# A fused recurrence and two expert mixtures: the first mixture's low weight halves and the logits' penalty moved from GpSimd to VectorE

## The chip, the core and the metric

One core of a Trainium2 chip runs the whole program as one launch. The metric is the device time of the launch in microseconds (us), as the median of several runs. Engines are named as the profile names them: PE is the matmul engine (TensorE) and PEld its weight loads, DVE is VectorE, ACT is ScalarE, POOL is GpSimd, SP is SyncE.

## The reference

Three stages work on 20224 tokens of 256 values, in float32.

```python
# 1. a gated recurrence over each of 4 sequences of 5056
f = lower_bound + (1 - lower_bound) * sigmoid(f_logit)
h = f[:, t] * h + (1 - f)[:, t] * x[:, t];  y[:, t] = h
# 2. first mixture: 8 experts, each takes exactly cap = 2528 tokens,
#    greedily by the sorted logits x @ w_gate
out[mask] = relu(x[mask] @ w1[e]) @ w2[e]          # w1: 256x1024, w2: 1024x256
# 3. second mixture: tokens with x @ w_skip > 0, each to its best expert
out[do] = xc + softmax_weight * (relu(xc @ w1[e]) @ w2[e])
```

## The kernel before

**Stages.** `attention` (L371) computes the recurrence and the first router's logits `L`, one value per token and expert. The first mixture follows, then the second. Each runs its experts one after the other.

**Split weights.** Every float32 weight is split into a high half, which is the value rounded to the matmul's format and is copied by ACT, and a low half, which is the value minus the high half. A product is three matmuls: high by high, low by high and high by low. The raw weights of one expert lie in `w1r` and `w2r`. The halves lie in two alternating sets, w10h, w10l, w20h, w20l and w11h, w11l, w21h, w21l, one for even and one for odd experts. `split_w` (L568) makes them in eight steps, four for w1 and four for w2, each of one ACT copy and one subtraction of 128x512. Its argument names the engine of the subtraction, but L579 sets it to POOL for the last four steps:

```python
        for h in range(DH):
            for c in range(0, F, F // 2):
                ...
                split_pool(w1h[:, h, s], w1l[:, h, s], w1r[:, h, s])
        eng = nc.gpsimd
        for a in range(0, FB, 2):
            split_pool(w2h[:, a:a + 2, :D], w2l[:, a:a + 2, :D], w2r[:, a:a + 2])
```

**Tiles of the first mixture.** An expert's tokens are five tiles of up to 512. A tile has eight slots `f` of 128 hidden values. In each slot, `up` (L875) issues six matmuls of 512 columns into a bank `hp`. ACT makes the high half `hh` of the relu, DVE the low half `hl`, which is the last reader of the bank. There are two such banks, so the `up` two slots later waits for this `hl`. `down` (L893) issues 12 matmuls for the slot two before. `gather` fetches the next tile's tokens with four indirect DMAs from POOL's queue, and after each tile `disp2` sends its rows out with eight indirect DMAs (`scatter`) from the same queue.

**Routing beside the tiles.** `route(k)` (L675) finds which tokens expert k takes, while expert k-1 computes. At its end it loads the expert's raw weights, takes the tokens out (`pn`, `apen`, `dl`), adds a large negative penalty to the chosen expert's logits (`L`, L796, one POOL instruction of 128x1264, for k below 6) and turns the choice into row numbers: `mstep` on DVE, three matmuls, then `cc`, `idf` and `idx`.

**Order.** The program is straight-line for each engine. What is interleaved goes by an estimate of when each engine gets to its work (class `Paced`). `route`, `prepare_w` (L836, the splits of expert k's weights, then `fold`, L843, which puts the second router's columns behind w2) and `prepare_2` (L827, the second mixture's first weights) are generators that yield conditions. `offer` (L929) goes on with each as long as `fits` says yes: a condition ("D", x) wants DVE's estimated end plus x to be at most PE's plus 3.0 us, ("A", x) the same for ACT with 1.0 us, ("R", t) wants t written. `prepare_w` asks for ("A", 0.5) and the raw weights, and for nothing of POOL. `until` (L1099) forces the generators on where a tile needs what they make. The first expert's weights are split before the first tile by `split_w(0, nc.vector)` (L1064). In the second mixture `ahead` (L1328) splits with `nc.gpsimd`.

Almost all of this stage is recorded under one line, L109, the pacing wrapper's, so the profile is read by tile names.

Of the kernel before, what the change touches and what calls it, by code (L numbers as in the profile page):

```python
# [20 lines left out]
class Paced:  # L21
    """nc, with an estimate of when each engine gets to what it was given: what is interleaved goes by it"""

# [18 lines left out]
    def look(self, table, ap):  # L42
        """the latest of the times that the table has for what overlaps ap"""
        lo, hi = self.span(ap)
        return max((t for (a, b), t in table.get(ap.name, {}).items() if a < hi and lo < b), default=0.0)
# [9 lines left out]
    def slot(self, tag, n, ap):  # L55
        """the tile ap takes the place of the one that had the tag n tiles ago"""
        old = self.banks.setdefault(tag, [])
        if len(old) >= n:
            self.book(self.w, ap[:], max(self.look(self.w, old[-n]), self.look(self.r, old[-n])))
        old.append(ap[:])  # L60
# [54 lines left out]
def attn_moe_moe2(ctx, tc, x, f_logit, lower_bound, g1, w1a, w2a, sk, g2, w1b, w2b, out):  # L115
# [35 lines left out]

# [1 line left out]
    jp = consts.tile([P, P], I32)  # L153
# [120 lines left out]
    def pick(a, b, k):  # L274
        """m: each token's best logit among the experts left, V: that one at its expert, else very low"""
        s = slice(a, b)
        n = b - a
        bc = [P, n, E]
        w8 = wE[:, None, :].to_broadcast(bc)
        nc.vector.tensor_reduce(m[:, s], L[:, s], axis=AX.X, op=OP.max)  # L280
        yield
        nc.vector.tensor_tensor(eqw[:, s], L[:, s], m[:, s, None].to_broadcast(bc), op=OP.is_equal)
        yield
        nc.vector.tensor_tensor(eqw[:, s], eqw[:, s], w8, op=OP.mult)
        yield
        nc.vector.tensor_reduce(ch[:, s], eqw[:, s], axis=AX.X, op=OP.max)
        if k:
            nc.vector.tensor_tensor(m[:, s], m[:, s], apen[:, s], op=OP.min)
        yield
        nc.vector.tensor_tensor(eqw[:, s], w8, ch[:, s, None].to_broadcast(bc), op=OP.not_equal)  # L290
        yield
        nc.vector.scalar_tensor_tensor(V[:, s], eqw[:, s], -2.0 * BIG, m[:, s, None].to_broadcast(bc),
                                       op0=OP.mult, op1=OP.add)
# [10 lines left out]
    def vt(g0, g1_, pt):  # L304
        """V's columns g0 * CG to g1_ * CG, experts along the partitions"""
        full = 0
        for g in range(g0, g1_):
            n = min(CG, C - g * CG)
            full += n == CG
            nc.tensor.transpose(pt[:n * E, (g - g0) * P:(g - g0 + 1) * P],  # L310
                                V[:, g * CG:g * CG + n, :].rearrange("p c e -> p (c e)"), ident)
        if full:
            nc.scalar.activation(VT[:, g0 * P:(g0 + full) * P], pt[:, :full * P], AF.Copy)
        if full < g1_ - g0:
            r = (C - (g1_ - 1) * CG) * E
            nc.scalar.activation(VT[:r, (g1_ - 1) * P:g1_ * P], pt[:r, full * P:(full + 1) * P], AF.Copy)

    def counts(v, TG):
        """how many of each partition's values reach the two values of TG"""
        n = v.free_size()  # L320
        cnt = rs.tile([P, 2], FT, name="cnt")
        nc.vector.tensor_scalar(junkd[:, :n], v, TG[:, 0, 0:1], 0.0, op0=OP.is_ge, op1=OP.add,
                                accum_out=cnt[:, 0:1])
        nc.scalar.activation(junka[:, :n], v, AF.Sign, bias=TG[:, 1, 0:1], scale=-1.0, accum_out=cnt[:, 1:2])
        return cnt
# [8 lines left out]
    def weigh(pc, rh, kc, LH, TG):  # L334
        """the fullest expert's count beside each value, and the ends LH moved to them"""
        pc3 = pc[:, :3 * E].rearrange("p (i e) -> p i e", i=3)
        nc.tensor.matmul(pc[:, :3 * E], ones, rh.rearrange("p i e -> p (i e)"), start=True, stop=False)
        nc.tensor.matmul(pc[:, :3 * E], ones, kc.rearrange("p i e -> p (i e)"), start=False, stop=True)
        nc.vector.tensor_reduce(TG[:, :, 1], pc3, axis=AX.X, op=OP.max)
        mk = rs.tile([P, 2, 2], I32, name="mk")  # L340
        nc.vector.tensor_scalar(mk[:, :, 0], TG[:, 0:2, 1], 0.0, None, op0=OP.is_ge)
        nc.vector.tensor_scalar(mk[:, :, 1], TG[:, 1:3, 1], 0.0, None, op0=OP.is_lt)
        for i in range(2):
            nc.vector.copy_predicated(LH, mk[:, i, :, None].to_broadcast([P, 2, 2]), TG[:, i:i + 2])

    def aim(LH, ca, cb):
        """the next two values: where a line between the ends would meet the wanted count, and a bit aside"""
        w = rs.tile([P, 1], FT, name="w")
# [12 lines left out]
    def ends(LH):  # L361
        """the first two values"""
        TG = rs.tile([P, 3, 2], FT, name="TG")
        nc.vector.tensor_copy(TG[:, 0::2, 0], LH[:, 0, 0:1].to_broadcast([P, 2]))
        dd = rs.tile([P, 1], FT, name="dd")
        nc.vector.tensor_tensor(dd, LH[:, 1, 0:1], LH[:, 0, 0:1], op=OP.subtract)
        nc.vector.scalar_tensor_tensor(TG[:, 1, 0:1], dd, -0.3, LH[:, 1, 0:1], op0=OP.mult, op1=OP.add)
        return TG
# [5 lines left out]
    def attention():  # L374
        with tc.tile_pool(name="a_in", bufs=3) as ain, tc.tile_pool(name="a_w", bufs=2) as aw, \
# [68 lines left out]
            def early(a, b):  # L444
                """the tokens' best experts, as far as they are known"""
                yield from pick(a, b, 0)
# [7 lines left out]
            def sample(b):  # L454
                """the first threshold as the first b columns would have it, and how far it may be off"""
                yield
# [111 lines left out]
    def split_w(q, eng):  # L568
# [5 lines left out]
        for h in range(DH):  # L574
            for c in range(0, F, F // 2):
                s = slice(c, c + F // 2)
                split_pool(w1h[:, h, s], w1l[:, h, s], w1r[:, h, s])
                yield
        eng = nc.gpsimd  # L579
        for a in range(0, FB, 2):  # L580
            split_pool(w2h[:, a:a + 2, :D], w2l[:, a:a + 2, :D], w2r[:, a:a + 2])
            yield

# [1 line left out]
    routed = {}  # L585
# [7 lines left out]
    def narrow(LH, tf, tiles, i):  # L593
        """one more value between the ends, on VectorE alone"""
        Z, Zt, Y, W, Wt, q, qi, c8, d1, mk = tiles
# [26 lines left out]
    def settle(LH):  # L622
        """where the rounds were not enough: some more, and then bit by bit"""
        tiles = [rs.tile([P, 32], FT, name="fZ", bufs=1), rs.tile([P, 32], FT, name="fZt", bufs=1),
# [16 lines left out]
    def bits(tf, tiles):  # L641
        """the greatest threshold that leaves some expert full, bit by bit, on VectorE alone"""
        Z, Zt, Y, W, Wt, q, qi, c8, _, _ = tiles
# [31 lines left out]
    def route(k):  # L675
        """a generator: yields the point of a slot at which it goes on"""
        last = k == E - 1
# [111 lines left out]
        if not last:  # L789
# [5 lines left out]
            if k < E - 2:  # L795
                nc.gpsimd.tensor_tensor(L, L, dl[:, None, :].to_broadcast([P, C, E]), op=OP.add)  # L796
        cc = rs.tile([P, 2, NJ], FT, name="cc")
# [29 lines left out]
    def prepare_2():  # L827
        load_raw(w1b[0], w2b[0])
        yield [("W", lambda: at[0] >= (E - 1) * TN * FB + 2)]
        step = split_w(0, nc.gpsimd)  # L830
        for _ in range(8):
            yield [("A", 0.5), ("R", w2r)]
            next(step, None)
        load_raw(w1b[1], w2b[1])

    def prepare_w(k):  # L836
        step = split_w(k % 2, nc.gpsimd)
        for _ in range(8):
            yield [("A", 0.5), ("R", w2r)]
            next(step, None)  # L840
        yield from fold(k % 2)

    def fold(q):  # L843
        """the second router's columns behind w2"""
        w2h, w2l = wts[q][1]
# [20 lines left out]

# [1 line left out]
    def xsplit_h(src, nb, off, h, xs):  # L868
# [42 lines left out]

# [1 line left out]
    TN = (NJ + 3) // 4  # L913
# [189 lines left out]

# [1 line left out]
    KT = 12  # L1105
# [30 lines left out]
    def tables():  # L1136
        nc.vector.tensor_tensor(cnt, base[0:1], bf0, op=OP.subtract)
        nc.vector.tensor_scalar(nti, cnt, float(T2 - 1), None, op0=OP.add)
        nc.vector.tensor_scalar(nti, nti, T2.bit_length() - 1, None, op0=OP.logical_shift_right)
        # a rest of up to P rows goes along with an earlier tile  # L1140
        nc.vector.scalar_tensor_tensor(wd[:, 0], nti, -1.0 * T2, cnt, op0=OP.mult, op1=OP.add)
# [14 lines left out]
        yield  # L1156
        # s2: the tile after the next expert's first
        g = s12[:, 2, :E - 1]
# [6 lines left out]
        yield  # L1165
        # nx[e, j + 1]: the second tile after tile j of expert e
        bc = [1, E, KT + 1]
# [108 lines left out]
    def broad(e, j):  # L1276
        """body, with the expert's last P rows beside the tile's"""
        q = e % 2
# [55 lines left out]

    # the first expert's first two tiles, from what the tiles before the last one sent it
    mt = bank()
# [111 lines left out]
```

## Time and profile before

| | us |
|---|---|
| median of 3 runs | 1945.02 (1944.35 to 1946.91) |
| span of the profiled execution | 2129.3 |
| attention, to the first matmul of the first mixture's `up` | 251.3 |
| first mixture, seven experts up to the eighth's first `up` | 251.3 to 1411.9 |

The profiled execution's own span is 184.3 us above the median of the unprofiled runs. The page doesn't show where that difference lies. Busy times are by engine. An idle time stands in brackets in the timeline, ahead of the instruction that ended it, with what released it.

### The profile page before, as it was taken

How to read it: one execution, taken by the hardware profiler on the slowest of the kernel's cores; microseconds unless marked ns; L12 is line 12 of the kernel's file. 1: busy time of each engine (PE TensorE's matmuls, PEld its weight loads, DVE VectorE, ACT ScalarE, POOL GpSimd, SP SyncE). 2: the span in 40 equal slices, each digit the busy share in tenths (PEclk: the TensorE clock that was granted, in tenths of full speed). 3: DMA queues.
4: the chain of work that ended last, by engine and by line, in shares of the span. 5: the costliest groups of instructions: out<-in, count | busy, mean ns of one | idle time of the engine just before them, and what ended most of it. 6: DMA issues, size and time to landing. Idle time of an engine off the chain costs nothing. (4 is left out here: it accounts for less than half of the span.)

```text
span 2129.3 us, 34969 instructions
## 1 busy us (share of the span) xinstructions
PE 1808.8 (85%) x12538; PEld 1663.9 (78%) x12538; DVE 1131.0 (53%) x3142; ACT 753.8 (35%) x1703; POOL 838.7 (39%) x847
## 2 busy tenths in 40 slices
PE   7994398898788789888797889888989999998998
PEld 6884277787677688777686778877879989998998
DVE  8999666666565666666565534332333333333332
ACT  4664243433433333433333443232222322223321
POOL 4552233542624443542634446354351322314311
PEclk9998699898889899998899999989999999999999
DMA  8999210212101110210201222011022323323222
GB/s 277 299 305 308 81 38 30 71 31 66 33 29 40 61 40 29 71 33 28 73 28 39 68 72 78 28 54 59 30 78 81 106 67 101 92 84 122 62 68 60
DMA packets 154181, 176.76 MB, mean 83 GB/s; under 512 B 17822, under 2 KB 129332, under 8 KB 153920
## 3 DMA queue, kind: packets, MB, share of 16 engines
q1 hardware_dynamic: 126800, 120.85, 18.8%
q0 software_dynamic: 27120, 52.76, 7.7%
q8 instruction: 124, 2.03, 0.4%
q14 instruction: 137, 1.12, 0.2%
HBM read 118.71 MB, written 76.34 MB: 92 GB/s over the span
## 5 line engine op out<-in xcount | busy, mean ns | idle before, releaser
L109 DVE SCALAR_TENSOR_TENSOR hl<-hp,hh 128x512 fp32r<-128x512 f32 (+2 forms) x480 | 322.8, 673 | 590.8 <-ACT hh L109 463.3
L109 ACT ACTIVATE hh<-hp 128x512 fp32r<-128x512 f32 (+2 forms) x480 | 280.4, 584 | 808.8 <-PE hp L109 581.7
L109 POOL DMA_INDIRECT buf_scr<-rt,ix x160 | 164.0, 1025 | 588.7 <-ACT hh L109 337.4
L109 PE MATMUL op<-w21h,hh 128*128 128x266 f32 (+1 forms) x960 | 262.4, 302 | 36.3 <-ACT rt L109 22.6
L109 PE MATMUL op<-w20h,hh 128*128 128x266 f32 (+1 forms) x960 | 261.9, 301 | 35.7 <-ACT rt L109 15.6
L109 PE MATMUL op<-w21l,hh 128*128 128x266 f32 (+1 forms) x960 | 255.6, 294 | 1.4 <-issue 1.4
L109 PE MATMUL op<-w20l,hh 128*128 128x266 f32 (+1 forms) x960 | 255.4, 294 | 0.0
L109 PE MATMUL hp<-xsh,w10h 128*128 128x256 f32 (+3 forms) x624 | 224.3, 369 | 29.2 <-DVE hl L109 13.7
L109 PE MATMUL hp<-xsh,w11h 128*128 128x512 f32 (+3 forms) x616 | 218.7, 365 | 27.8 <-DVE hl L109 21.5
L109 POOL DMA_INDIRECT out_dram<-xg,tin x85 | 83.7, 985 | 392.8 <-DVE xg L109 324.6
L109 PEld LDWEIGHTS op<-w21h,hh 128*128 128x128 f32 x960 | 189.7, 198 | 46.8 <-ACT rt L109 25.0
L109 PEld LDWEIGHTS op<-w20h,hh 128*128 128x128 f32 x960 | 189.4, 197 | 44.4 <-issue 19.6
L109 PE MATMUL hp<-xsh,w10l 128*128 128x256 f32 (+3 forms) x624 | 214.3, 353 | 0.4 <-issue 0.4
L109 PE MATMUL hp<-xsh,w11l 128*128 128x512 f32 (+3 forms) x616 | 210.0, 350 | 0.0
L109 PEld LDWEIGHTS op<-w21l,hh 128*128 128x128 f32 x960 | 189.7, 198 | 5.4 <-issue 0.8
L109 PEld LDWEIGHTS op<-w20l,hh 128*128 128x128 f32 x960 | 189.7, 198 | 5.0
L109 POOL DMA_INDIRECT xg<-y_scr,idx x160 | 167.5, 1047 | 59.9 <-issue 46.1
L109 POOL DMA_INDIRECT out_dram<-rt,ix x160 | 158.1, 988 | 48.8 <-issue 48.2
L109 PE MATMUL hp<-xsl,w10h 128*128 128x256 f32 (+3 forms) x624 | 167.7, 350 | 2.5 <-DVE txi L109 1.5
L109 PE MATMUL op<-w20h,hl 128*128 128x266 f32 (+1 forms) x960 | 164.0, 294 | 3.4 <-issue 3.3
L109 PE MATMUL op<-w21h,hl 128*128 128x266 f32 (+1 forms) x960 | 163.2, 294 | 1.9 <-issue 1.8
L109 PE MATMUL hp<-xsl,w11h 128*128 128x512 f32 (+3 forms) x616 | 164.0, 348 | 0.0
(372 smaller groups left out, 3543.1 us busy)
## 6 DMA issues: line engine op xcount, KB each, us to landing
ft<-in_f_logit_dram SPq DMA_DIRECT2D x39, 512.0 KB
xt<-in_x_dram SPq DMA_DIRECT2D x39, 512.0 KB
y_scr<-yt SPq DMA_DIRECT2D x78, 256.0 KB
w1r<-in_moe_w_dram SPq DMA_DIRECT2D x16, 1024.0 KB
w2r<-in_moe_w_dram SPq DMA_DIRECT2D x16, 1024.0 KB
rt<-buf_scr SPq DMA_DIRECT2D x42, 258.0 KB
xg<-buf_scr SPq DMA_DIRECT2D x40, 258.0 KB
xg<-y_scr,idx POOLq DMA_INDIRECT x160
```

What stands on the lines that cost most here:

```text
L109: return f(*a, **k)
```

## The change

In the first mixture all eight low halves of an expert's weights are subtracted on VectorE. L579 goes, so the engine handed to `split_w` holds for w2 too, and `prepare_w` and `prepare_2` hand it VectorE. Each of their eight steps now also asks for ("D", 0.7). The penalty on `L` runs on VectorE for k = 1 to 5, on GpSimd still for k = 0. `ahead`, in the second mixture, is as before. The diff also takes out doc strings and comments, which are left out here.

```diff
@@ def split_w
                 split_pool(w1h[:, h, s], w1l[:, h, s], w1r[:, h, s])
                 yield
-        eng = nc.gpsimd
         for a in range(0, FB, 2):
@@ def route
             if k < E - 2:
-                nc.gpsimd.tensor_tensor(L, L, dl[:, None, :].to_broadcast([P, C, E]), op=OP.add)
+                (nc.vector if k else nc.gpsimd).tensor_tensor(L, L, dl[:, None, :].to_broadcast([P, C, E]), op=OP.add)
@@ def prepare_2
-        step = split_w(0, nc.gpsimd)
+        step = split_w(0, nc.vector)
         for _ in range(8):
-            yield [("A", 0.5), ("R", w2r)]
+            yield [("A", 0.5), ("D", 0.7), ("R", w2r)]
             next(step, None)
@@ def prepare_w
-        step = split_w(k % 2, nc.gpsimd)
+        step = split_w(k % 2, nc.vector)
         for _ in range(8):
-            yield [("A", 0.5), ("R", w2r)]
+            yield [("A", 0.5), ("D", 0.7), ("R", w2r)]
             next(step, None)
```

## Rows read from the trace of the kernel before

**Rows 1.** The page's first line.
```profile
span 2129.3 us, 34969 instructions
```

**Rows 2.** Expert 1's stretch: PE, PEld, DVE, ACT, POOL busy, then PEclk, DMA.
```profile
416.00:584.00 168.00, 140.98 (x898) 125.62 (x898) 101.81 (x322) 62.46 (x149) 74.86 (x73) 0.91 0.14 44
```

**Rows 3.** PE's waits, 260 to 1330 us: in total, times, longest.
```profile
PE hp L109 <- DVE hl L109: 34.8, 12, 10.8
PE ms L109 <- DVE mstep L109: 32.1, 8, 10.1
```

**Rows 4.** Timeline, expert 2's weights: start, duration, instruction, idle before it.
```profile
545.15 4.94 POOL L109 TENSOR_TENSOR w10l<-w1r,w10h 128x512 fp32r<-128x512 f32 x4
545.49 9.15 DVE L109 SCALAR_TENSOR_TENSOR idf<-cc 128x6 f32<-128x6 f32 x1
550.04 4.57 POOL L109 TENSOR_TENSOR w20l<-w2r,w20h 128x512 fp32r<-128x512 f32 x4
555.79 0.77 PE L109 MATMUL hp<-xsh,w11h 128*128 128x480 f32 x1 [10.83 <-DVE hl L109]
```

**Rows 5.** Timeline, the same place for experts 3, 4 and 5.
```profile
735.00 0.90 PE L109 MATMUL ms<-dX,mstep 128*128 128x160 f32 x3 [8.12 <-DVE mstep L109]
884.95 7.36 DVE L109 TENSOR_SCALAR mstep<-iot,b 128x384 fp32r<-128x384 f32 x1
892.46 0.90 PE L109 MATMUL ms<-dX,mstep 128*128 128x160 f32 x3 [7.75 <-DVE mstep L109]
1052.27 9.03 DVE L109 TENSOR_SCALAR mstep<-iot,b 128x384 fp32r<-128x384 f32 x1
1061.45 0.90 PE L109 MATMUL ms<-dX,mstep 128*128 128x160 f32 x3 [10.13 <-DVE mstep L109]
```

**Rows 6.** Four DVE tiles: durations min/median/max in ns, first and last start.
```profile
L109 DVE SCALAR_TENSOR_TENSOR idf<-cc x21: 159/174/9154, 241.7 to 1277.4; 128x6 f32<-128x6 f32 x7, 128x14 f32<-128x14 f32 x7, 128x3 f32<-128x3 f32 x5, 128x4 f32<-128x4 f32 x1
L109 DVE TENSOR_SCALAR mstep<-iot,b x56: 279/412/9226, 238.5 to 1274.7; 128x384 fp32r<-128x384 f32 x47, 128x256 fp32r<-128x256 f32 x7, 128x512 fp32r<-128x512 f32 x1, 128x128 fp32r<-128x128 f32 x1
L109 DVE TENSOR_TENSOR apen<-apen,pn x7: 324/325/1273, 238.0 to 1191.0; 128x158 f32<-128x158 f32 x7
L109 DVE TENSOR_SCALAR dl<-dl x7: 171/172/1121, 238.4 to 1191.4; 128x8 f32<-128x8 f32 x7
```

**Rows 7.** Stretches of 6.5 us just after PE went on; PEclk is third from last.
```profile
556.00:562.50 6.50, 6.50 (x25) 5.99 (x26) 3.13 (x10) 2.14 (x8) 3.68 (x4) 0.57 0.29 81
735.00:741.50 6.50, 6.50 (x33) 6.29 (x34) 4.05 (x13) 2.99 (x12) 3.85 (x4) 0.68 0.29 83
893.00:899.50 6.50, 6.50 (x37) 6.29 (x37) 1.19 (x4) 4.71 (x18) 3.30 (x4) 0.76 0.30 83
1062.00:1068.50 6.50, 6.50 (x28) 6.02 (x28) 2.19 (x5) 2.86 (x11) 3.29 (x4) 0.63 0.30 84
```

**Rows 8.** Groups over the span by shape: busy, mean ns of one, idle before.
```profile
L109 DVE TENSOR_TENSOR w10l<-w1r,w10h 128x512 fp32r<-128x512 f32 x4 | 2.5, 686 | 0.2 <-issue 0.2
L109 DVE TENSOR_TENSOR eqw<-L,m 128x1264 f32<-128x1264 f32 x6 | 8.8, 1474 | 0.2
```

**Rows 9.** Timeline, an undisturbed slot: `hl`, and the next `up` into its bank.
```profile
1193.75 0.69 DVE L109 SCALAR_TENSOR_TENSOR hl<-hp,hh 128x512 fp32r<-128x512 f32 x1 [1.86 <-ACT w10h L109]
1196.93 0.40 PE L109 MATMUL hp<-xsh,w11h 128*128 128x512 f32 x1
```

**Rows 10.** Timeline, start of the first mixture: DVE's low halves beside POOL's gathers.
```profile
242.27 2.50 DVE L109 TENSOR_TENSOR w10l<-w1r,w10h 128x512 fp32r<-128x512 f32 x4 [0.24 <-issue]
242.31 1.75 POOL L109 DMA_INDIRECT xg<-y_scr,idx  x1 [0.62 <-DVE idx L109]
251.25 1.50 DVE L109 TENSOR_TENSOR xsl<-ms,xsh 128x512 fp32r<-128x512 f32 x2 [5.27 <-ACT xsh L109]
```

**Rows 11.** Timeline, expert 2: `fold`'s last instruction, and the first `up`.
```profile
575.42 0.24 DVE L109 TENSOR_TENSOR w20l<-wt,w20h 128x80 fp32r<-128x80 f32 x1 [0.34 <-issue]
583.73 0.50 PE L109 MATMUL hp<-xsh,w10h 128*128 128x512 f32 x1 [1.43 <-issue]
```

## The prediction

> **What bounds the kernel now.** I read the page first, then the busy times by stretch, then PE's waits, and last the timeline around the longest of them. The profiled execution spans 2129.3 us [rows 1], against a median of 1945.0. The reader should see in the stretch of one expert [rows 2] that PE is busy 141.0 of 168.0 us at a mean granted clock of 0.91, DVE 101.8, ACT 62.5 and POOL 74.9. PE sets the time, in program order, and 27.0 us of this stretch are its waits. POOL, the engine that the change relieves, is busy less than half, and none of PE's waits names it: the two largest that name an engine are DVE's `hl`, 34.8 us in 12 waits, and DVE's `mstep`, 32.1 us in 8 [rows 3]. Each has one wait of over 10 us, and that is where to look.
>
> In the timeline of the longest [rows 4], DVE's `idf`, on six elements, takes 9.15 us. It starts 0.34 us after POOL has begun a run of eight low halves and ends at 554.64, within 0.03 us of the run's end (550.04 + 4.57 = 554.61). PE has stood for 10.83 us by then. For experts 3, 4 and 5 it is `mstep` that lasts 9.2, 7.36 and 9.03 us, with PE waiting 8.12, 7.75 and 10.13 us [rows 5]. Undisturbed, `idf` takes 0.17 and `mstep` 0.41 us by their medians, and the longest of each is the one beside the run [rows 6]. So four of PE's waits come from DVE instructions that cannot get on while POOL subtracts, and nothing in PE's list of waits says POOL.
>
> The Trainium skill (SBUF — State Buffer, Who interferes with whom) says that VectorE's second memory port pair is GpSimd's only one, and that whoever issues second blocks until the first instruction is finished. The engines agree, the length doesn't: one instruction of the run is about 1.2 us, and `idf` waited for eight. By the rule alone the four waits would be worth some 5 us; by the rows they are worth their full length, and the rows decide.
>
> **The change part by part**, in us of the profiled execution.
>
> 1. *POOL's runs of low halves go.* The four waits are 10.83 + 8.12 + 7.75 + 10.13 = 36.8.
>
> 2. *The clock behind them.* After each wait PE goes on at half the clock for a while: over the next 6.5 us the granted clock is 0.57, 0.68, 0.76 and 0.63, between its levels of 1.2 and 2.4 GHz [rows 7]. PE is busy throughout, so it loses 6.5 x (0.43 + 0.32 + 0.24 + 0.37) = 8.8. If PE doesn't stand, this goes too.
>
> 3. *Expert 1.* There the same contention stretches `apen` from 0.32 to 1.27 and `dl` from 0.17 to 1.12 [rows 6], both on the way to an `mstep` that PE waits for: 1.9. Together 36.8 + 8.8 + 1.9 = 47.5.
>
> 4. *What is next at the four places.* At expert 2 PE stopped at 555.79 - 10.83 = 544.96. Without the stall DVE does `idf`, the copy to `idx` (taken as `idf`), `mstep` and `hl`: 545.49 + 0.17 + 0.17 + 0.41 + 0.69 = 546.9, so 2.0 of the wait stays. At expert 3 PE stopped at 726.88, after `mstep` would have ended: 0. At expert 4 it stopped at 884.71 and `mstep` would end at 885.36: 0.7. At expert 5, at 1051.32 and 1052.68: 1.4. Back come 4.1.
>
> 5. *The low halves on DVE.* An expert's eight take 8 x 0.686 = 5.5 [rows 8], for experts 1 to 7 and the second mixture's first: 64 of them, 43.9 of DVE time. Their cover is the spare time of `hl`. In an undisturbed slot `hl` ends at 1194.44 and the `up` that takes its bank starts at 1196.93 [rows 9], so 2.5 us of other work may stand before it. The new condition ("D", 0.7) lets a step go only while DVE's estimate is within 3.0 - 0.7 = 2.3 us of PE's: up to four in a row, 2.7. That is just about the spare, so low halves alone cost nothing, but beside the router's `mstep` or `cc` some will be late. Nothing in the trace shows this mixture of work, so the bounds are 0 and all of it, 43.9. I take two of eight as exposed, 1.4 per expert, 11.0 in all: nearer to the lower end, because DVE has 66 us free in an expert's stretch [rows 2]. DVE's load hardly rises: 43.9 come, and about 34 of stalls go. The ACT copies stay as many as they were. What is queued behind a waiting step on DVE is the next `hl`, and for that PE waits.
>
> 6. *The penalty on DVE.* Five instructions of the size of `eqw`, 1.47 each [rows 8], between `dl` and the next `mstep`. For experts 2 to 5 DVE is waiting for ACT after it; for expert 1 PE stands at that `mstep`, so 1.5 is on the path. Bounds 0 and 7.4. `pick` reads the result later, on the same engine.
>
> 7. *At nothing.* The first expert's four w2 halves, 2.7 on DVE, fall into the 5.27 us in which DVE waits before the first `xsl` [rows 10]; without that cover they would cost 2.7. POOL's queue gets about 80 us emptier, so gathers and scatters move ahead, and nobody on PE's path waited for them. The loads of the next raw weights wait for the last reader of `w1r` and `w2r`, which will be DVE, sooner than POOL.
>
> The sum: 47.5 - 4.1 - 11.0 - 1.5 = 30.9 saved. The extra 184.3 us of the profiled execution can't be placed. The stalls last as long as POOL's run, whatever PE's speed, so I take them at face value: 1945.0 - 30.9 = 1914.1. Scaled by 1945.0 / 2129.3 the saving would be 28.2, or 1916.8.
>
> **The rivals.**
>
> *A. Slower: DVE's own chores hold `hl`.* Place: the tile before each expert change, where the router's tail, the low halves and `hl` share one queue. Price: up to 43.9 + 7.4. It turns the sign when over 43.4 of these 51.3 us are exposed, five sixths. At full price the time is 1945.0 - 43.4 + 51.3 = 1952.9. For it speaks that `hl` is already PE's largest named wait; against it, the 2.5 us of spare and the 66 us free. Chance 0.08.
>
> *B. No change: the weights come late.* With the new condition the steps go out more slowly, and `fold` comes behind them. `fold` ends at 575.66 and expert 2's first `up` is at 583.73 [rows 11], a margin of 8.1. Each us of delay beyond it is one us of PE at each of five or so experts, so some 14 us of delay eat the saving of 30.9 (5 x 6), and the time is 1945. Against it: DVE is free for four tenths of a stretch [rows 2], so 5.5 us of low halves find room within some 14 us, and POOL's eight, 9.5 us in a row, are no earlier done today. Chance 0.08.
>
> *C. Contention in the other direction: a low half on DVE is held by POOL's indirect DMAs, as `idf` was by the run.* If each of the 64 were held for one gather of up to 1.75 us [rows 10], DVE would lose 112 us, and at the share exposed in step 5, a quarter, 28 us of the path: 1942.1. Against it: four low halves ran beside that very gather in 2.50 us, 0.63 apart, and it was the gather that was long. The Trainium skill's rule speaks for it: in the section named above, a VectorE instruction with both inputs in that memory contends with a GpSimd instruction that reads it. Chance 0.07.
>
> **How the numbers follow.** The forecast, stalls gone and part of the low halves exposed, has 0.77: 1914.1, with its own range from 1945.0 - 47.5 = 1897.5 (nothing comes back) to 1937 (22.9 more exposed than I took: three quarters of the low halves). A, B and C have the rest. The range of 8 in 10 is the forecast's with a few us below, for stretches of other DVE instructions beside POOL that I have not counted: 1893 to 1938; it leaves out A, B and C's upper part. This kernel can be told from no change at about 0.2%, 3.9 us: faster 0.77 + 0.05 of C and B = 0.82, same 0.09 from B and C, slower 0.09 from A and what C could grow to.
>
> **What would show it.** Right: no DVE instruction of the first mixture over 2 us, `idf` near 0.17 and `mstep` near 0.41 us at most; the waits on `mstep` falling from 32.1 to under 8; the stretches of experts 1 to 4, in which the four waits lie, shrinking by some 6 to 10 each, the others hardly. Step 5 is wrong if the waits on `hl` outside the four places grow by more than 11 or shrink; rival B, if PE stands at an expert's first `up`; C, if low halves on DVE are over 0.7. The forecast falls if PE's waits of 8 to 11 us stay with another name on them.

## The result, and the profile after

The changed kernel takes 1899.89 us (median of 4 runs, 1897.61 to 1900.46) beside 1945.97 of the kernel before on the same chip (4 runs): a ratio of 0.976, with a 95% interval of 0.9746 to 0.9774. It saves 46.1 us; 30.9 were forecast, with 1893 to 1938 as the range.

The profiled execution of the changed kernel begins its page with

```profile
span 1897.9 us, 34994 instructions
...
PE 1735.7 (91%) x12538; PEld 1613.8 (85%) x12538; DVE 1133.1 (60%) x3215; ACT 757.9 (40%) x1703; POOL 748.1 (39%) x774
```

where [rows 1] has 2129.3 us: PE is busy for nine tenths of the span.

One condition has to be known to read what follows: in the profiled execution of before that the prediction rests on, and in the first and third group of experiments, PE in many tiles also stood or ran slowly, in part for reasons that the profile gives no releaser for (52.3 us of PE's idle time in the first mixture of `before` end with `issue`, none in `before_third`; before took 2149 and 2119 us in those groups), so kernels are compared only within a group. The two kernels are laid side by side by two traces of the second group: `before_third`, which is the kernel before once more, and `after_again`, the changed one.

PE's waits in the first mixture, from the first `up` of its first expert to the start of the second mixture, in total, times and longest; first the kernel before (`before_third`):

```profile
PE ms L109 <- DVE mstep L109: 27.4, 9, 8.1
PE hp L109 <- DVE hl L109: 12.2, 5, 10.6
...
PE op L109 <- ACT rt L109: 7.8, 4, 3.8
PE ms L109 <- DVE xsl L109: 2.5, 1, 2.5
```

and the same list of the changed kernel (`after_again`):

```profile
PE ms L109 <- DVE rh L109: 12.5, 5, 2.8
PE ms L109 <- DVE mstep L109: 9.7, 4, 5.7
...
PE hp L109 <- DVE hl L109: 1.9, 5, 0.4
...
PE op L109 <- ACT rt L109: 0.7, 1, 0.7
```

These answer to [rows 3]. The waits on `hl` and `mstep` fall by 28.0, the waits on `rt` by 7.1. What is at the top now, `rh`, is a wait of the router's rounds, 11.9 us before.

Busy times by stretch, in `before_third`: two experts (the columns are those of [rows 2]), then the first mixture and the second.

```profile
398.30:547.50 149.20, 134.34 (x897) 121.15 (x896) 107.86 (x323) 62.47 (x148) 73.50 (x71) 0.94 0.16 49
834.60:985.90 151.30, 136.92 (x902) 123.11 (x900) 104.70 (x319) 61.92 (x145) 75.81 (x74) 0.94 0.15 49
249.60:1383.00 1133.40, 1060.92 (x7083) 957.30 (x7083) 719.43 (x2249) 465.19 (x1103) 578.77 (x556) 0.96 0.17 54
1383.00:1944.20 561.20, 519.35 (x4146) 514.67 (x4144) 202.05 (x444) 161.51 (x326) 159.16 (x150) 0.97 0.29 86
```

The same four in `after_again`:

```profile
401.20:535.60 134.40, 131.24 (x898) 119.15 (x897) 99.59 (x327) 61.53 (x145) 62.93 (x62) 0.99 0.18 55
805.70:941.00 135.30, 132.30 (x897) 120.09 (x897) 99.64 (x327) 61.47 (x145) 62.68 (x62) 0.97 0.18 55
250.80:1331.70 1080.90, 1047.29 (x7083) 950.20 (x7083) 709.99 (x2318) 467.06 (x1103) 487.54 (x484) 0.98 0.18 57
1331.70:1896.70 565.00, 520.41 (x4146) 515.18 (x4144) 201.92 (x444) 161.56 (x326) 159.19 (x150) 0.97 0.29 85
```

The first mixture is 52.5 us shorter. With the same 7083 matmuls PE's idle time falls from 1133.40 - 1060.92 = 72.5 to 33.6 us, by 38.9, and its busy time by 13.6, at a granted clock that rises from 0.96 to 0.98. The stretch before it grows by 1.2 and the second mixture by 3.8, so 47.5 of span are left. DVE, which got 69 instructions and some 51 us of work more (64 x 0.686 + 5 x 1.47), is busy 9.4 us *less*: the stalls counted as its busy time.

DVE's tiles in `after_again`, as in [rows 6] and, for the low half, [rows 8]:

```profile
L109 DVE SCALAR_TENSOR_TENSOR idf<-cc x21: 159/167/175, 240.1 to 1106.0; 128x6 f32<-128x6 f32 x7, 128x14 f32<-128x14 f32 x7, 128x3 f32<-128x3 f32 x5, 128x4 f32<-128x4 f32 x1
...
L109 DVE TENSOR_SCALAR mstep<-iot,b x56: 279/412/650, 237.0 to 1103.3; 128x384 fp32r<-128x384 f32 x47, 128x256 fp32r<-128x256 f32 x7, 128x512 fp32r<-128x512 f32 x1, 128x128 fp32r<-128x128 f32 x1
...
L109 DVE TENSOR_TENSOR w20l<-w2r,w20h x20: 651/684/693, 244.4 to 1223.7; 128x512 fp32r<-128x512 f32 x20
```

The longest `idf` is 0.18 us instead of 9.15 and the longest `mstep` 0.65 instead of 9.23. The low halves of `w20l` on DVE take at most 0.69 us beside what POOL still has, its DMAs above all; of all four low tiles the longest is 0.72.

Of the waits on `hl` and `mstep`, what is left is mostly at one place, expert 1's weights. DVE's timeline there (start, duration, instruction, idle before it), and PE's two waits behind it:

```profile
366.52 0.69 DVE L109 TENSOR_TENSOR w11l<-w1r,w11h 128x512 fp32r<-128x512 f32 x1 [1.83 <-ACT w11h L109]
...
367.40 0.33 DVE L109 TENSOR_TENSOR apen<-apen,pn 128x158 f32<-128x158 f32 x1
...
367.84 0.17 DVE L109 TENSOR_SCALAR dl<-dl 128x8 f32<-128x8 f32 x1
...
368.04 1.47 DVE L109 TENSOR_TENSOR L<-L,dl 128x1264 f32<-128x1264 f32 x1
369.44 0.69 DVE L109 TENSOR_TENSOR w11l<-w1r,w11h 128x512 fp32r<-128x512 f32 x1
370.04 0.42 DVE L109 TENSOR_SCALAR mstep<-iot,b 128x384 fp32r<-128x384 f32 x1
...
370.60 0.90 PE L109 MATMUL ms<-dX,mstep 128*128 128x160 f32 x3 [5.66 <-DVE mstep L109]
...
374.68 0.93 PE L109 MATMUL ms<-dX,mstep 128*128 128x160 f32 x3 [3.18 <-DVE mstep L109]
```

Two low halves and the penalty stand ahead of the `mstep` that PE waits for, and the first of them first waits 1.83 us for ACT's high half.

### The profile page after: what moved, and what is told of

Its sections match the earlier page's. It is cut to its first block, busy times and chain, and to the rows that moved or that the text cites. A ratio compares the mean times of both kernels' runs of the same rounds, so it can differ in the third digit from the quotient of the medians.

```text
span 1897.9 us, 34994 instructions
## 1 busy us (share of the span) xinstructions
PE 1735.7 (91%) x12538; PEld 1613.8 (85%) x12538; DVE 1133.1 (60%) x3215; ACT 757.9 (40%) x1703; POOL 748.1 (39%) x774
## 5 line engine op out<-in xcount | busy, mean ns | idle before, releaser
L109 PE MATMUL op<-w20h,hh 128*128 128x266 f32 (+1 forms) x960 | 254.9, 295 | 23.3 <-PEq L1382 11.0
L109 PE MATMUL op<-w21h,hh 128*128 128x266 f32 (+1 forms) x960 | 252.8, 293 | 13.9 <-PEq L1382 8.8
L109 PE MATMUL op<-w20l,hh 128*128 128x266 f32 (+1 forms) x960 | 249.3, 289 | 0.0
L109 PE MATMUL op<-w21l,hh 128*128 128x266 f32 (+1 forms) x960 | 247.3, 287 | 0.0
L109 PE MATMUL hp<-xsh,w10h 128*128 128x256 f32 (+3 forms) x624 | 215.2, 355 | 1.3 <-DVE hl L109 0.8
L109 PE MATMUL hp<-xsh,w11h 128*128 128x512 f32 (+3 forms) x616 | 212.5, 354 | 1.3 <-DVE hl L109 1.1
L109 PE MATMUL hp<-xsh,w10l 128*128 128x256 f32 (+3 forms) x624 | 207.3, 342 | 0.0
L109 PEld LDWEIGHTS op<-w21h,hh 128*128 128x128 f32 x960 | 182.7, 190 | 21.1 <-issue 11.1
L109 PEld LDWEIGHTS op<-w21l,hh 128*128 128x128 f32 x960 | 183.0, 191 | 5.1
L109 PE MATMUL op<-w20h,hl 128*128 128x266 f32 (+1 forms) x960 | 158.0, 287 | 0.0
```

Of the source, the lines that this page charges most:

```text
L109: return f(*a, **k)
```

## The experiments

**Group 1: the change taken apart.** The theory is that PE stood because DVE could not run beside POOL's subtractions. The rival is that something else that the change moves did it: the penalty, or the load of the queues. `before_again` is the kernel before, for the waits under this group's condition.

> The kernel before, once more, for a second trace. If the 184 us by which its first profiled execution exceeded the median belong to that execution alone, the span here is near 1946 and the four waits of PE behind POOL's runs of low halves (36.8 us in the first trace) are still there. If they belong to profiling this kernel, the span is near 2129 again.

It took 2151.38 us. The four waits are there again: 10.48, 8.12, 7.75 and 10.14, beside 10.83, 8.12, 7.75 and 10.13 in the trace that the prediction rests on [rows 4, 5]. They belong to the program, not to one execution, though the size of two of them changes, as group 2 shows.

`halves_only` is the changed kernel with the penalty left on POOL:

```diff
-                (nc.vector if k else nc.gpsimd).tensor_tensor(L, L, dl[:, None, :].to_broadcast([P, C, E]), op=OP.add)
+                nc.gpsimd.tensor_tensor(L, L, dl[:, None, :].to_broadcast([P, C, E]), op=OP.add)
```

> The changed kernel with the logits' penalty back on GpSimd for every k; the low halves stay on VectorE. Theory (the gain is the end of VectorE's stalls beside GpSimd's run of eight subtractions): 1900 to 1906, since one penalty of 2.97 us is a much shorter run. Rival (the penalty's 2.97 us stall is a good part): 1915 or more.

It took 2136.77 us beside before's 2148.89, 0.994 (0.9914 to 0.9966); a second time, in group 3, 0.991 (0.9884 to 0.9935). The waits beside runs of low halves are gone, but each of the five penalties on POOL now holds a DVE instruction. In `halves_only`'s timeline at expert 1:

```profile
390.06 3.21 POOL L109 TENSOR_TENSOR L<-L,dl 128x1264 f32<-128x1264 f32 x1 [6.52 <-DVE dl L109]
390.48 3.00 DVE L109 TENSOR_SCALAR mstep<-iot,b 128x384 fp32r<-128x384 f32 x1
...
393.63 0.90 PE L109 MATMUL ms<-dX,mstep 128*128 128x160 f32 x3 [6.71 <-DVE mstep L109]
```

`mstep` ends 0.21 us after the penalty and has taken 3.00 us instead of 0.41. At the next four experts the same instruction stretches a low half on DVE, two of them together to 4.46, or an `idf` to 0.99. By its time the run sides with the rival, which wanted 1915 or more of 1946, a ratio of 0.984 or more. The waits on `hl` and `mstep` fall from 61.5 us in `before_again` to 30.1, but those on `rh` rise from 33.5 to 52.3; why they rise is not shown.

`penalty_only` is the kernel before with only the penalty moved:

```diff
-                nc.gpsimd.tensor_tensor(L, L, dl[:, None, :].to_broadcast([P, C, E]), op=OP.add)
+                (nc.vector if k else nc.gpsimd).tensor_tensor(L, L, dl[:, None, :].to_broadcast([P, C, E]), op=OP.add)
```

> The kernel before with only the logits' penalty on VectorE for k = 1 to 5. Theory: 1940 to 1947, the runs of eight and their stalls stay. Rival (the penalty ahead of the run is what lets it collide with idf and mstep): 1930 or less. The prediction's step 6 would have it slower by 1.5, 1947.

It took 2177.54 us, 1.012 (1.0087 to 1.0154): slower. Its timeline at expert 2 shows the old stall:

```profile
548.77 4.93 POOL L109 TENSOR_TENSOR w10l<-w1r,w10h 128x512 fp32r<-128x512 f32 x4
548.91 8.40 DVE L109 TENSOR_SCALAR mstep<-iot,b 128x384 fp32r<-128x384 f32 x1
...
553.65 3.44 POOL L109 TENSOR_TENSOR w20l<-w2r,w20h 128x512 fp32r<-128x512 f32 x3
...
557.46 0.90 PE L109 MATMUL ms<-dX,mstep 128*128 128x160 f32 x3 [9.38 <-DVE mstep L109]
```

Against the rival: the penalty alone gains nothing, the runs of low halves are what PE waits for. It was expected level and is slower. Its waits behind the runs, 9.38, 7.34, 7.98, 6.95 and 5.26, are 36.9 us, as much as the four of `before_again`, 36.5: a run of eight at expert 6's weights is a fifth place now. So the slowdown lies elsewhere, and stays open.

`halves_twice` is the changed kernel with every low half on DVE computed a second time, unknown to the estimate that orders the work:

```diff
             eng.tensor_tensor(lo, src, hi, op=OP.subtract)
+            if eng is nc.vector:
+                nc.nc.vector.tensor_tensor(lo, src, hi, op=OP.subtract)
```

> The changed kernel with each of the 68 low halves on VectorE subtracted twice in a row, without telling the pacing estimate: 46.6 us more of VectorE work in the same places. If the low halves lie in the spare time of hl: 1900 to 1906. If a quarter is exposed, as the prediction's step 5 took: 1911. If VectorE sets the time there (rival A): 1930 to 1946.

It took 2123.69 us, 0.987 (0.9835 to 0.9903), which would be faster than `halves_only`; in group 3 it took 2108.40, 0.996 (0.9935 to 0.998), slower than `halves_only` there. By time it is inconclusive. By the traces, some 44 us more on DVE in the first mixture (64 x 0.686) change the waits on `hl` and `mstep` together from 30.1 to 29.2 us against `halves_only` in this group, and from 23.8 to 33.0 in the second try; at expert 1 they are 6.78 and 3.91 beside 5.66 and 3.18 in `after_again`. A quarter exposed, as step 5 has it, would be 11.0; these waits give at most 9.2. It is no clean price: `halves_only` differs in the penalty too, and the changed kernel itself did not run in these groups.

**Group 2: what of the saving is the engine, and what the pacing.** Before took 1943.42 us here (1937.89 to 1945.63, 7 runs). The theory says that a POOL subtraction holds DVE wherever it stands; the rival says that only the run of eight is bad, and that offering them singly on POOL would do.

> The kernel before, for a trace beside the changed kernel's on the same chip. The theory wants the four waits of PE behind POOL's runs of low halves here too, 30 to 40 us in all.

> The changed kernel once more, beside the kernel before on the same chip. Where the kernel before takes 1946 it should take 1900 as measured; where the kernel before takes some 2149, with PE idle or at half clock for other reasons, the theory (four stalls of 8 to 11 us and the half clock behind them go) gives 25 to 46 less, 2103 to 2124.

They took 1946.01 (one run) and 1897.25 us, the latter 0.9759 (0.9743 to 0.9776). Their traces are those of the section above. In `before_third`, at expert 2:

```profile
508.08 11.92 DVE L109 SCALAR_TENSOR_TENSOR idf<-cc 128x6 f32<-128x6 f32 x1
...
510.52 4.91 POOL L109 TENSOR_TENSOR w10l<-w1r,w10h 128x512 fp32r<-128x512 f32 x4
...
515.40 4.57 POOL L109 TENSOR_TENSOR w20l<-w2r,w20h 128x512 fp32r<-128x512 f32 x4
...
521.15 0.77 PE L109 MATMUL hp<-xsh,w11h 128*128 128x480 f32 x1 [10.62 <-DVE hl L109]
```

`idf` ends at 520.00, the run at 519.97. The four waits are 10.62, 8.13, 4.69 and 5.80 here, 29.2 in all.

`no_backlog` is the changed kernel without the new condition, so the engine changes and the pacing doesn't (the line stands in `prepare_2` and in `prepare_w`):

```diff
-            yield [("A", 0.5), ("D", 0.7), ("R", w2r)]
+            yield [("A", 0.5), ("R", w2r)]
```

> The changed kernel without the new condition on VectorE's backlog: low halves on VectorE, offered by ScalarE's backlog alone as before, up to eight in a row (5.5 us). If the backlog condition matters: 5 to 20 us slower than the changed kernel, in waits on hl. If the engine alone matters: within 4 us of it.

It took 1914.93 us (1911.27 to 1915.89), 0.9852 (0.9836 to 0.9868). Of the 46.2 us of this group the two moves to DVE alone give 28.5, and the condition 17.7 more. The stretches of experts 2 to 5 are 139 to 140 us, in `after_again` 134 to 136. In its timeline at expert 4's weights:

```profile
777.43 1.29 DVE L109 TENSOR_TENSOR w10l<-w1r,w10h 128x512 fp32r<-128x512 f32 x2
...
778.33 3.70 POOL L109 DMA_INDIRECT buf_scr<-rt,ix  x1 [14.85 <-ACT xsh L109]
778.64 2.49 DVE L109 TENSOR_TENSOR w20l<-w2r,w20h 128x512 fp32r<-128x512 f32 x4
```

and at expert 3's first tile:

```profile
684.91 0.35 POOL L109 MEMSET rt<- 128x268 f32 x1
...
685.29 0.39 ACT L109 ACTIVATE rt<-op 96x266 f32<-96x266 f32 x1 [3.88 <-POOL rt L109]
...
685.73 0.41 PE L109 MATMUL op<-w21h,hh 128*128 128x266 f32 x1 [2.38 <-ACT rt L109]
```

Here six low halves go out in a row, and now it is POOL that is held: a scatter of 1.0 us takes 3.70 and ends 0.90 after the last of them (778.64 + 2.49 = 781.13). Waits on `hl` rise to 4.7 us, and those on `rt` to 10.4, from 0.7: `rt` is cleared by a POOL MEMSET that stands in POOL's queue behind scatters and gathers, and these are late. The scatters ahead of it begin 6.8 us before expert 3's first `up`, in `after_again` 10.4 us before it, and two of them take 2.09 and 1.62 us, beside DVE's router work and not beside low halves; so the scatter of 3.70 us is not what PE waits for here. That MEMSET starts 10.7 us after expert 3's first `up` (674.21), in `after_again` 5.6 us after it (671.39):

```profile
677.00 0.34 POOL L109 MEMSET rt<- 128x268 f32 x1
```

`pool_singly` is the kernel before with its low halves on POOL held back by POOL's own backlog:

```diff
-            yield [("A", 0.5), ("R", w2r)]
+            yield [("A", 0.5), ("G", 1.5), ("R", w2r)]
@@ fits
+        if kind == "G":
+            return nc.t["G"] + x <= now
```

> The kernel before with its low halves still on GpSimd, but offered by GpSimd's own estimated backlog, so that few of them follow one another; the penalty stays on GpSimd too. If the row of eight is what hurts, a single subtraction stalls VectorE for at most 1.3 us, within the 2.5 us of spare, and most of the gain is there: within 12 us of the changed kernel. If any subtraction on GpSimd hurts, or GpSimd is too full to spread them, it stays within 12 us of the kernel before.

It took 1972.74 us, 1.0152 (1.0135 to 1.0169): slower, not faster, and outside both ranges that were expected. The four old waits are gone, but new ones stand in their place; its list of PE's waits begins with

```profile
PE ms L109 <- DVE rh L109: 47.3, 11, 9.5
PE ms L109 <- DVE wt L109: 30.5, 9, 13.7
```

and in its timeline, just before expert 2's first `up` at 571.37, stands

```profile
549.73 6.08 DVE L109 TENSOR_SCALAR rh<-mask,cnt 128x16 f16<-128x16 f32 x2
549.75 2.49 POOL L109 TENSOR_TENSOR w10l<-w1r,w10h 128x512 fp32r<-128x512 f32 x2
...
552.20 3.43 POOL L109 TENSOR_TENSOR w20l<-w2r,w20h 128x512 fp32r<-128x512 f32 x3
...
555.86 0.20 PE L109 MATMUL ms<-rh,ones 128*128 128x24 f16 x1 [9.50 <-DVE rh L109]
...
560.55 1.18 POOL L109 TENSOR_TENSOR w20l<-w2r,w20h 128x512 fp32r<-128x512 f32 x1 [4.92 <-ACT w20h L109]
...
561.12 0.71 DVE L109 TENSOR_SCALAR mk<-TG 128x2 int32<-128x2 f32 x2
```

The last low half is done at 561.73, in `before_third` at 519.98, 27.5 us before its expert. So late, they meet the next expert's routing rounds and `fold` (`wt`), which PE waits for. Five still go in a row, and one alone still stretches a pair of `mk` on two elements from 0.24 us, in the round before, to 0.71. Lateness and contention are mixed in this kernel, so it doesn't price a single subtraction. It does show that holding them back on POOL in this way is no way to the gain; whether single subtractions on POOL, in time, would reach it stays open.

**Group 3: the place that is left.** Before took 2118.63 us here (13 runs). `halves_only_2` and `halves_twice_2` repeat the kernels of group 1, and are told there.

> The changed kernel with the logits' penalty back on GpSimd, once more, beside the others of this group. A penalty on GpSimd is one instruction of 2.97 us, which in the earlier trace held VectorE's next instruction for up to 3.9 us at five places. If hl's 2.5 us of spare covers it: within 3 us of the changed kernel (1895 to 1900). If the rest of each stall is exposed: 1.4 us at each of five places and the clock behind them, 1904 to 1910.

> The changed kernel with each low half subtracted twice, 46.6 us more of VectorE work, beside the others of this group. PE waits 1.9 us for hl in the changed kernel's first mixture, so VectorE has room: 1897 to 1903, that is at most a seventh of the added work exposed. A quarter exposed, as step 5 took it: 1909. All of it exposed (rival A): 1940.

`router_first` is the changed kernel with the penalty moved to the end of `route`, and expert 1's splits held until its router is through:

```diff
@@ route
-            if k < E - 2:
-                (nc.vector if k else nc.gpsimd).tensor_tensor(L, L, dl[:, None, :].to_broadcast([P, C, E]), op=OP.add)
+            if k == 0:
+                nc.gpsimd.tensor_tensor(L, L, dl[:, None, :].to_broadcast([P, C, E]), op=OP.add)
...
+        if 0 < k < E - 2:
+            yield [("D", 1.4)]
+            nc.vector.tensor_tensor(L, L, dl[:, None, :].to_broadcast([P, C, E]), op=OP.add)
@@ prepare_w
+        if k == 1:
+            yield [("W", lambda: routed[k][2] >= 4)]
```

> The changed kernel with two things moved in VectorE's order: the penalty goes to the end of the routing of an expert, behind the last mstep, and expert 1's low halves start only when its first row numbers are known. In the changed kernel PE waits 5.66 and 3.18 us for two mstep of expert 1, behind one penalty (1.47) and three low halves (2.06). If those are the cause: 3 to 6 us faster than the changed kernel, 1891 to 1894. If the low halves then come too late for expert 1's first up (PE waits there instead): within 2 us of it or slower.

It took 2075.27 us, 0.9801 (0.9777 to 0.9825), the fastest of the group. The changed kernel itself was not run in this group, so the timed gain over it is open; what can be read is expert 1's place:

```profile
383.04 0.54 PE L109 MATMUL ms<-dX,mstep 128*128 128x160 f32 x3 [1.36 <-DVE mstep L109]
...
385.70 0.56 PE L109 MATMUL ms<-dX,mstep 128*128 128x160 f32 x3 [2.13 <-DVE mstep L109]
```

The waits of 5.66 and 3.18 are 1.36 and 2.13, though across two groups: 5.35 us were due to what stood ahead of `mstep`. The penalty's duration is 1.47 of it, which leaves an estimated 3.9 for low halves with their wait for ACT; the two were moved together.

`router_first_both` also has the second mixture's low halves on DVE:

```diff
-            for _ in split_w((e + 1) % 2, nc.gpsimd):
+            for _ in split_w((e + 1) % 2, nc.vector):
```

> As router_first, and the second mixture's low halves on VectorE too, where VectorE is busy for about a third of the time and GpSimd's runs of eight stretch the copy to tin to between 0.9 and 2.7 us. If those stretches matter: 2 to 6 us faster than router_first. In the trace PE's waits there are behind branches and not behind VectorE, so the likelier answer is within 2 us of it.

It took 2076.99 us, 0.9814 (0.9791 to 0.9836), no different from `router_first`. Runs of low halves on POOL cost nothing that can be measured in the second mixture: DVE is busy there for 202 of 565 us, a third, and of PE's 34.8 us of idle time there in `before_third` 27.9 are behind its own sequencer and 2.7 behind DVE.

## Why the prediction was right, and where its sum was off

The forecast (faster, by the stalls that go) held, and the time lies in its range. The sum was 30.9 of saving; the two spans differ by 47.5. The 16.6 between them split up by the windows: idle time 38.9 where the sum has 36.8 + 1.9 - 4.1 - 11.0 - 1.5 = 22.1, the clock 13.6 where it has 8.8, and 5.0 lost outside the first mixture, where it has nothing. Within the idle time step 1 counted 7.6 us too much, waits of 13.4 us that were no term went too, and steps 3 to 6 gave back 29.2 + 13.4 - 38.9 = 3.7 us, where the sum has 14.7. That the time lies in the range is in part luck: the first two errors have opposite signs.

*Step 1, the runs* was right: all four waits are gone, and `penalty_only`, which keeps the runs, keeps stalls of 5 to 9 us beside them. Its size was not: the four are worth 29.2 in `before_third`, not 36.8. The stall at experts 4 and 5 depends on how far POOL's run has got when `mstep` begins, and that differs between the two traces. So "at face value" was the wrong choice for this term, and scaling by the spans, 33.6, would not have been enough.

What it left out is larger than that error. The fall of 39 us in named waits is `mstep` 17.7, `hl` 10.3, `rt` 7.1 and `xsl` 3.9. The `rt` waits were no term at all, nor were those on `xsl`, the longest of which follows a DVE `ex` of 4.98 us beside four low halves on POOL. Step 7 names the emptier POOL queue and says that nobody on PE's path waited for it; but `rt`, a result tile, is cleared by a MEMSET in that queue, so PE did, by way of ACT. One of PE's waits for `mstep` was of that kind too: in `before_third` a DVE `ex` on 32 columns takes 4.44 us beside the penalty and a low half on POOL, and PE waits 2.43 behind it. So `rt`, `xsl` and this one are the 13.4 us above.

*Step 2, the clock* was right in its mechanism and too small: PE's busy time for the same matmuls falls by 13.6. It counted 6.5 us behind each of four waits and nothing behind the others that went.

*Step 3* was right: `apen` and `dl` take 0.33 and 0.17 us. But PE's wait at that place grew, 1.20 + 2.69 + 2.13 = 6.0 before, 5.66 + 3.18 = 8.8 after, because steps 5 and 6 put their cost at just that place.

*Step 4, what is next* was too high. The waits on `mstep` other than expert 1's are 9.7 - 8.8 = 0.9 us, and those on `hl` 1.9 in all, so at most 2.8 of the 4.1 stayed.

*Step 5, the low halves on DVE* is the term that was most off: 11.0 against the estimated 3.9 at expert 1, and what part of the 1.9 on `hl` is theirs. By its own mark it stands, since the waits on `hl` outside the four places went from 1.6 to 1.9; its size does not. A quarter exposed came from comparing four low halves, 2.7 us, with the 2.5 us to spare, as if the condition let four through beside a late `hl`. It doesn't: in the changed kernel they go out one to three at a time, once four, where DVE is ahead. Nor do they need `hl`'s spare time when they replace stalls: DVE's busy time in the mixture falls by 9.4. What the step didn't see is that a low half waits for ACT's high half, 1.83 us, with `mstep` queued behind it.

*Step 6, the penalty* has the duration right, 1.47 us ahead of PE's `mstep` at expert 1; its own share of the wait was not measured. That it stands in a place of its own was wrong: it belongs with the low halves. On POOL it holds DVE as they did (`halves_only`). That the gain needs both parts is likely and not shown, since the changed kernel did not run beside `halves_only`.

*What has no price in it* is the condition on DVE's backlog. The prediction used it only to ask how many low halves may go in a row and, in rival B, how late they get. `no_backlog` prices it at 17.7 us of the 46.2; between the two traces, 12.8 us apart, the waits on `rt` make 9.7 and those on `hl` 2.8. It is no further addend, because step 5 supposes the condition: it is what would have come back without it.

*The rivals.* A, DVE's chores holding `hl`, would have shown as longer waits on `hl`: 1.9 us in five. B, late weights, is excluded by expert 2's last `fold` instruction (527.72 + 0.24) against its first `up` at 535.58, a margin of 7.6 us, [rows 11] has 8.1. C, a low half held by POOL's DMAs, is excluded by its longest, 0.72 us. The contention is there, but it is the DMA that waits, up to 3.70 us in `no_backlog`: it costs POOL's queue. That any of it reached PE is not shown: at expert 4's weights the queue then stands idle for 10.81 us before the scatters of the next tile.

*The marks.* No DVE instruction of the first mixture is over 2 us, as stated. The waits on `mstep` fell to 9.7, not under 8: expert 1's place. The stretches of experts 1 to 4 shrank by 14.9, 11.1, 5.9 and 16.0, three of them by more than the 6 to 10 stated. Expert 5's shrank by 9.1 too, where hardly anything was stated, and expert 6's grew by 3.6, with 14 matmuls more in it: some work moved from the one into the other.

Of the Trainium skill's rule (SBUF — State Buffer, Who interferes with whom), which the prediction weighed: for a lone instruction rule and row now agree, one penalty of 3.21 us held one `mstep` for 3.00. For a run they mostly differ: `idf` was held for all eight, to within 0.03 us of the run's end. Three instructions of `before_third` did get in after one subtraction of a run, as the rule has it (last section).

What stays open: why `penalty_only` is slower than before, and the 3.8 us that the second mixture lost with unchanged work. Of the 3.8, 2.3 lie in one wait of PE: 4.71 us without a releaser at 1424.40 in `after_again`, where `before_third` has 2.37 at 1473.24.

## What to carry to other kernels

Read the longest duration of each small VectorE instruction beside its median: a stall through GpSimd is booked as VectorE's busy time, and PE's list of waits names VectorE and not GpSimd. Work that two engines can do may belong on the one that does it faster, also if that one is the busier, and it should be offered by that engine's backlog: here a low half took 0.69 us instead of 1.2 to 1.3, the engine gave 28.5 us and the pacing 17.7. When stalls go, look at every queue that they had delayed, and at who takes a buffer from it.

## What the runs showed of the hardware

Beside a run of GpSimd subtractions without a gap, a VectorE instruction was mostly held to the end of the run, not of one subtraction: `idf` on six elements took 11.92 us, where the penalty and eight low halves followed each other. In `before_third` seven instructions were held over two or more subtractions to the run's end. Three others got in between two subtractions of a run, such as `po` here, at 790.32, just after the penalty's end (787.26 + 3.01 = 790.27) and with two low halves following at once:

```profile
787.26 3.01 POOL L109 TENSOR_TENSOR L<-L,dl 128x1264 f32<-128x1264 f32 x1 [7.89 <-DVE dl L109]
...
788.70 1.62 DVE L109 TENSOR_TENSOR po<-po,ob 128x32 f32<-128x32 f32 x1
...
790.23 2.53 POOL L109 TENSOR_TENSOR w10l<-w1r,w10h 128x512 fp32r<-128x512 f32 x2
```

What decides between the two stays open. How small the held instruction is makes no difference (`mk`, on two elements, up to 2.58 us instead of 0.17 in `pool_singly`).

In the other direction, runs of six subtractions on VectorE held a GpSimd indirect DMA at two places of `no_backlog`, 3.70 us instead of 1.0; beside a third such run, at expert 3's weights, two of these DMAs took 1.29 and 1.47. So in either direction a run without a gap can be dear, many times what one subtraction costs, and is not so each time.
